# A larger first block, early multiplications and a split last tile in a gated mix of attention and a gMLP block

## The chip, the cores and the metric

The kernel runs on one core of a Trainium2 chip. The metric is device time in microseconds (us), the median of several executions of the same program. A profile is one further execution, with every instruction and every DMA packet recorded. The engines are named as in the profile: PE (TensorE, the matrix multiplications), PEld (its weight loads), DVE (VectorE), ACT (ScalarE), POOL (GpSimd) and SP (SyncE). In this kernel SP issues every transfer. The matrix engine writes only to PSUM, which is used as eight banks of 128 x 512 float32 numbers.

## What is computed

There are 2048 tokens (S) of width 1024 (D), in bfloat16. Two branches of the same input x are mixed by a gate of each token:

```python
x = A_x
g = _sigmoid((x * gate_w).sum(-1, keepdims=True))
a = _A_ref(x, A_wqkv, A_wo)      # dilated sliding-window attention, 32 heads of 32, 8 positions each
b = _B_ref(x, B_w_in, B_w_sp, B_b_sp, B_w_out)
return g * a + (1 - g) * b

# _B_ref
z = _gelu(jnp.einsum('bsd,df->bsf', x, w_in))        # w_in: 1024 x 3584, Fh = 1792
z1 = z[..., :Fh].copy()
z2 = _layernorm(z[..., Fh:], axis=-1)
g = jnp.einsum('ts,bsf->btf', w_sp, z2) + b_sp[None, :, None]
return jnp.einsum('bsf,fd->bsd', z1 * g, w_out)
```

## The kernel before, in words

Work is tiled by 128 tokens (row tiles i = 0 to 15) and by 128 of the 1024 input features (k tiles kt = 0 to 7). `xT` holds x transposed, features on the partitions. `w2` holds the second half of w_in in four column blocks c of 512, 512, 512 and 256 columns (`ZC`, `ZW`), and the gate's weights as one more column of the last block.

The order of PE's work is the order in which the program writes it:

1. Row tiles 0 and 1 are transposed on PE (`z2_pair`, L230), because x arrives in plain layout for these two; DVE and ACT copy the results into `xT` (L234, L236). Then these two row tiles are multiplied with column block 0 of `w2` (L215), interleaved by pairs of k tiles so that each of four transfers of `w2` (L389, two k tiles of 512 columns, 256 KB) feeds four multiplications.
2. Row tiles 2 to 15 are multiplied with column block 0 (`z2_tile`). Their `xT` comes from transposing DMAs (L394), which SP issues after the transfers above.
3. The q, k and v projections of eight groups of four heads (L421); ACT copies the results out, SP stores them to DRAM and loads them back in the attention's layout.
4. The remaining z2 tiles (`z2_tile(i, c)` for c = 1 to 3, L441), with the sum of squares of each row tile on ACT (L443).
5. z1 by gelu (L463), stored to DRAM.
6. The spatial product (`g_chunk`, L477), two chunks, then alternately with `final_chunk` (L498 attention output times wo, L502 gated product times w_out), which mixes the two (ACT L505, DVE L506) and stores one output tile of 128 x 1024 (L509).

The attention itself runs on DVE (L257 to L296), beside all this. Its steps are placed into the program by a planner, `Beat`. Each stage of PE work reports its columns with `beat.run(cols)`, at 2360 columns a us; steps with a due time are emitted once the planner's clock has reached it. The attention's due times hang on the clock at the start of stage 3: `attention_steps(beat.now + QKV_US + 10.0)` (L410). At its end it loads wo (L348) and the first transposed attention outputs `oT` (L351), which stage 6 needs. SP works through its instructions in order, so a transfer that waits holds back those behind it.

PSUM tiles are taken in turn from one pool of eight, whatever their use.

Of the kernel before, what the change touches and what calls it, by code (L numbers as in the profile page):

```python
# [10 lines left out]
F32 = mybir.dt.float32  # L11
BF = mybir.dt.bfloat16

P = 128
S = 2048
D = 1024
KT = D // P
# [8 lines left out]
FH = 1792  # L26
NF = FH // P
ZC = 512
ZW = (512, 512, 512, 256)
# [21 lines left out]
def kernel(  # L51
# [13 lines left out]
    nc = tc.nc  # L65
    x2 = A_x.rearrange("b s d -> (b s) d")
    out2 = out.rearrange("b s d -> (b s) d")

    apool = ctx.enter_context(tc.tile_pool(name="arena", bufs=1))
    sm = ctx.enter_context(tc.tile_pool(name="small", bufs=1))  # L70
    psum = ctx.enter_context(tc.tile_pool(name="psum", bufs=8, space=bass.MemoryType.PSUM))
# [4 lines left out]
    def reg(off, n):  # L76
        return arena[:, off:off + n]
# [3 lines left out]
    v_d = dpool.tile([NG, S + 16, C], BF, name="v_d")  # L81
    z1_d = dpool.tile([4, P, NF * 512], BF, name="z1_d")
    o_d = dpool.tile([S, D], BF, name="o_d")

    ident = sm.tile([P, P], BF, name="ident")
    make_identity(nc, ident[:])
# [3 lines left out]
    for jh in range(2):  # L90
        for w in range(W):
            n = min(8, max(0, 14 - 2 * w - 8 * jh))
# [4 lines left out]
    g_s = sm.tile([P, 16], F32, name="g_s")  # L97
    gl_s = sm.tile([P, 16], F32, name="gl_s")
    omg = sm.tile([P, 16], F32, name="omg")
# [17 lines left out]
    w_out_sb = reg(X_OFF, NF * D).rearrange("p (f n) -> p f n", f=NF)  # L117
# [5 lines left out]
    wo_sb = reg(A_OFF, KT * D).rearrange("p (k n) -> p k n", k=KT)  # L123
    oT_slots = [reg(A_OFF + 8192 + r * 1024, 1024).rearrange("p (k t) -> p k t", k=KT) for r in range(3)]
    ob_slots = [reg(A_OFF + 11264 + r * 1024, 1024) for r in range(3)]
    asb_slots = [reg(A_OFF + 14336 + r * 1024, 1024).bitcast(F32) for r in range(2)]
    w2 = reg(CD_OFF, KT * W2P).rearrange("p (k c) -> p k c", k=KT)
# [16 lines left out]
    win_v = B_w_in.rearrange("(k p) c -> p k c", p=P)  # L144
    wsp_v = B_w_sp.rearrange("(a t) s -> a t s", t=P)
    wo_v = A_wo.rearrange("(g h d) n -> g h d n", g=NG, h=HG, d=DH)
    sync = nc.sync
# [38 lines left out]
    beat = Beat()  # L186
# [19 lines left out]
    def z2_tile(i, c):  # L206
        N = ZW[c] + 1 if c == 3 else ZW[c]
        ps = psum.tile([P, 512], F32, name="ps", tag="ps")
        for kt in range(KT):
            z2_mm(ps, i, c, kt, N)  # L210
        z2_out(ps, i, c)
        beat.run(KT * N)

    def z2_mm(ps, i, c, kt, N):
        nc.tensor.matmul(ps[:, 0:N], xT[:, kt, i * P:(i + 1) * P], w2[:, kt, ZC * c:ZC * c + N],  # L215
                         start=(kt == 0), stop=(kt == KT - 1))

    def z2_out(ps, i, c):
        n = ZW[c]
        nc.scalar.activation(z2[:, i, ZC * c:ZC * c + n], ps[:, 0:n], ACT.Gelu_apprx_tanh,  # L220
                             accum_out=s1[:, 4 * i + c:4 * i + c + 1])
        if c == 3:
            nc.scalar.copy(gl_s[:, i:i + 1], ps[:, n:n + 1])

    def z2_pair():
        for i in range(2):
            for h in range(2):
                pt = psum.tile([P, 4, P], BF, name="pt", tag="ps")
                for k in range(4):
                    nc.tensor.transpose(pt[:, k, :], xn[:, i, (4 * h + k) * P:(4 * h + k + 1) * P], ident[:])  # L230
                for k in (0, 2):
                    dst = xT[:, 4 * h + k:4 * h + k + 2, i * P:(i + 1) * P]
                    if k == 0:
                        nc.vector.tensor_copy(dst, pt[:, k:k + 2, :])  # L234
                    else:
                        nc.scalar.copy(dst, pt[:, k:k + 2, :])  # L236
        pair = [psum.tile([P, 512], F32, name="ps", tag="ps") for _ in range(2)]
        for kk in range(0, KT, 2):
            for i in range(2):
                for kt in (kk, kk + 1):  # L240
                    z2_mm(pair[i], i, 0, kt, ZW[0])
        for i in range(2):
            z2_out(pair[i], i, 0)
        beat.run(2 * KT * ZW[0])

    L = att_L
    L4 = L[:].rearrange("p (a w n) -> p a w n", a=2, w=W, n=32)
# [102 lines left out]
    def load_oT(a):  # L350
        sync.dma_start_transpose(oT_slots[a % 3], o_d[a * P:(a + 1) * P, :])  # L351

    def stats(i):
        sl = slice(i - 3, i + 1)
        s1v = s1[:, 4 * (i - 3):4 * (i + 1)].rearrange("p (i c) -> p i c", c=4)
        nc.vector.tensor_reduce(mean[:, sl], s1v, AX.X, ALU.add)
        nc.vector.tensor_scalar(mean[:, sl], mean[:, sl], 1.0 / FH, None, ALU.mult)
        nc.vector.tensor_tensor(var[:, sl], mean[:, sl], mean[:, sl], ALU.mult)
        nc.vector.scalar_tensor_tensor(var[:, sl], s2[:, sl], 1.0 / FH, var[:, sl], ALU.mult, ALU.subtract)
        nc.vector.tensor_scalar(var[:, sl], var[:, sl], 0.0, EPS, ALU.max, ALU.add)  # L360
        nc.gpsimd.tensor_tensor(rstd[:, sl], var[:, sl], cm05[:, sl], ALU.pow)
        beat.on_vector(0.8)

    def norm(ii):
        nc.vector.tensor_scalar(z2[:, ii, :], z2[:, ii, :], mean[:, ii:ii + 1], rstd[:, ii:ii + 1],
                                ALU.subtract, ALU.mult)
        beat.on_vector(0.75)
# [17 lines left out]

    for i in range(2):
        sync.dma_start(xn[:, i, :], x_v[:, i, :])  # L387
    for kk in range(0, KT, 2):
        sync.dma_start(w2[:, kk:kk + 2, 0:ZC], win_v[:, kk:kk + 2, FH:FH + ZC])  # L389
    for i in range(2, 16):  # L390
        if i == 14:
            load_w(0, 3)
# [3 lines left out]
    load_wg(1)  # L396
    for t_d in (k_d, v_d):
        sync.dma_start(bass.AP(tensor=t_d.tensor, offset=t_d.offset, ap=[[16, P], [(S + 16) * C, NG], [1, 16]]), zeros[:])
    for c in range(1, 4):
        sync.dma_start(w2[:, :, ZC * c:ZC * c + ZW[c]], win_v[:, :, FH + ZC * c:FH + ZC * c + ZW[c]])  # L400
    sync.dma_start(w2[:, :, FH:FH + 1], gw_v)

    z2_pair()
    for i in range(2, 16):
        if i == 14:
            v_order(0)
# [6 lines left out]
    for g in range(NG):  # L413
# [3 lines left out]
        for j in range(NJ):  # L417
            ps = psum.tile([P, 512], F32, name="ps", tag="ps")
            for kt in range(KT):
                lhsT = _sub_ap(xT_flat, kt * S + j, [[NJ, P]])  # L420
                nc.tensor.matmul(ps[:, 0:3 * C].rearrange("p (t c) -> p t c", t=3), lhsT, wgt[:, 0:3, kt, :],  # L421
                                 start=(kt == 0), stop=(kt == KT - 1))
# [15 lines left out]
    load_w1(0)  # L438
    load_w1(1)
    for i in range(16):  # L440
        for c in range(1, 4):  # L441
            z2_tile(i, c)
        nc.scalar.activation(junk, z2[:, i, :], ACT.Square, accum_out=s2[:, i:i + 1])  # L443
        if i % 4 == 3:
            beat.at(beat.now + 6.0, lambda i=i: stats(i))
            for ii in range(i - 3, i + 1):
                beat.at(beat.now + 11.0, lambda ii=ii: norm(ii))
# [6 lines left out]
    for f in range(NF):  # L454
# [5 lines left out]
        for c in range(4):  # L460
            ps = psum.tile([P, 512], F32, name="ps", tag="ps")
            for kt in range(KT):
                nc.tensor.matmul(ps[:], w1[:, kt, (f % 4) * P:(f % 4 + 1) * P], xT[:, kt, 512 * c:512 * (c + 1)],  # L463
                                 start=(kt == 0), stop=(kt == KT - 1))
# [22 lines left out]
    def final_chunk(c):  # L487
        z1c = z1c_slots[c % 2]
        for aa in range(4):
            a = 4 * c + aa  # L490
            oT = oT_slots[a % 3]
            ob = ob_slots[a % 3]
            if a > 0 and a + 2 < 16:
                load_oT(a + 2)
            for n in range(2):
                psa = psum.tile([P, 512], F32, name="psa", tag="ps")
                for kt in range(KT):
                    nc.tensor.matmul(psa[:], oT[:, kt, :], wo_sb[:, kt, 512 * n:512 * (n + 1)],  # L498
                                     start=(kt == 0), stop=(kt == KT - 1))
                psb = psum.tile([P, 512], F32, name="psb", tag="ps")  # L500
                for f in range(NF):
                    nc.tensor.matmul(psb[:], z1c[:, f, aa * P:(aa + 1) * P], w_out_sb[:, f, 512 * n:512 * (n + 1)],  # L502
                                     start=(f == 0), stop=(f == NF - 1))
                asb = asb_slots[n]
                nc.scalar.activation(asb, psa[:], ACT.Copy, scale=g_s[:, a:a + 1])  # L505
                nc.vector.scalar_tensor_tensor(ob[:, 512 * n:512 * (n + 1)], psb[:], omg[:, a:a + 1], asb,  # L506
                                               ALU.mult, ALU.add)
                beat.run((KT + NF) * 512)
            sync.dma_start(out2[a * P:(a + 1) * P, :], ob)  # L509

    load_z1c(0)
    for aa in range(4):
# [7 lines left out]
    for aa in range(4):  # L520
        load_wsp(3, aa)
    beat.flush(1e9)
    final_chunk(0)
    load_z1c(2)
    g_chunk(2)
    final_chunk(1)
    load_z1c(3)
    g_chunk(3)
    final_chunk(2)
    final_chunk(3)  # L530

# [29 lines left out]
```

## Time and profile before

| what | value |
|---|---|
| median of 3 runs | 718.73 us (718.09 to 718.87) |
| profiled execution, its own time | 718.52 us |
| its span, first to last instruction | 716.7 us |
| PE busy | 709.1 us, 99% of the span |
| DVE, ACT busy | 414.2 us, 251.7 us |
| mean rate of the DMAs | 130 GB/s |
| PE idle before its first instruction | 3.6 us |
| last multiplication ends | 712.9 us from the span's start |

The span begins with the first instruction that the profile shows and ends with the last one; 1.8 us of the execution's own time lie around it. Where a group of multiplications gives a mean of 379 ns for 128 x 512, that is the time of one from issue to its modelled end; they overlap, and the distance from one start to the next is shorter. That distance, not the mean, is what a multiplication costs in a row of them.

### The profile page before, as it was taken

To read this page: it belongs to the slowest core of one execution; us is meant where nothing else is said; L and a number is where in the kernel's file an instruction comes from. 1 tells how busy PE (TensorE), PEld (TensorE's weight loads), DVE (VectorE), ACT (ScalarE), POOL (GpSimd) and SP (SyncE) were. 2 spreads that over 40 slices of the span, in tenths; PEclk is the share of its full clock that TensorE was granted. 3 is DMA by queue.
4 is the path that set the end of the run, shared out by engine and by line. 5 is a ranking of instruction groups with operands and counts; after the bars stand their busy time and mean duration, and the time that the engine had idled before them with its cause. 6 is when DMAs were issued, how large, how long until landed. Compare 5 with 4: busy or idle time off the path is not lost.

```text
span 716.7 us, 8882 instructions
## 1 busy us (share of the span) xinstructions
PE 709.1 (99%) x3600; PEld 400.2 (56%) x3600; DVE 414.2 (58%) x427; ACT 251.7 (35%) x482; POOL 11.5 (2%) x23
## 2 busy tenths in 40 slices
PE   7999999999999999999999999999999999999997
PEld 3488888888865554444444444444444444444443
DVE  0001979999999999999999996211222112221111
ACT  4444455444378894343522111111111111111111
POOL 1000000000000021000000000000000000000000
PEclk9999999999999999999999999999999999999999
DMA  9978687667681207953469764482400223002210
GB/s 212 178 205 232 144 205 180 162 152 176 176 247 55 85 6 206 265 189 119 142 211 278 267 118 138 84 146 59 133 1 0 54 55 113 1 1 59 59 45 29
DMA packets 177449, 92.93 MB, mean 130 GB/s; under 512 B 145024, under 2 KB 168576, under 8 KB 176896
## 3 DMA queue, kind: packets, MB, share of 16 engines
q1 hardware_dynamic: 177408, 92.36, 49.0%
q8 instruction: 28, 0.46, 0.3%
q14 instruction: 13, 0.11, 0.1%
HBM read 47.71 MB, written 28.38 MB: 106 GB/s over the span
## 4 chain that ended last, share of the span: by engine, by line
PE 99%; DMA 1%; SPq 0%; DVE 0%; issue 0%; DVEq 0%
PE ps L477 27%; PE ps L421 23%; PE ps L215 14%; PE psb L502 13%; PE ps L463 13%; PE psa L498 8%; DMA arena<-in_B_w_in_dram 1%; SPq L387 0%; DVE arena L506 0%; DVEq L506 0%
## 5 line engine op out<-in xcount | busy, mean ns | idle before, releaser
L477 PE MATMUL ps<-arena 128*128 128x512 bf16 x896 | 193.9, 379 | 0.0
L421 PE MATMUL ps<-arena 128*128 128x384 bf16 x1024 | 166.6, 326 | 0.0
L421 PEld LDWEIGHTS <-arena 128*128 128x128 bf16 x1024 | 147.6, 144 | 18.9
L477 PEld LDWEIGHTS <-arena 128*128 128x128 bf16 x896 | 87.7, 98 | 105.7
L502 PE MATMUL psb<-arena 128*128 128x512 bf16 x448 | 101.9, 379 | 0.0
L215 PE MATMUL ps<-arena 128*128 128x512 bf16 (+1 forms) x512 | 99.0, 356 | 0.2 <-DMA arena<-in_B_w_in_dram 0.2
L463 PE MATMUL ps<-arena 128*128 128x512 bf16 x448 | 96.9, 379 | 0.0
L506 DVE SCALAR_TENSOR_TENSOR arena<-psb,omg,arena 128x512 bf16<-128x512 f32 x32 | 24.0, 751 | 125.9 <-PE psb L502 125.9
L257 DVE TENSOR_TENSOR arena<-arena 128x8192 bf16<-128x8192 bf16 x16 | 70.8, 4423 | 43.8 <-DMA arena<-k_d 43.5
L424 ACT CAST arena<-ps 128x384 bf16<-128x384 f32 x128 | 60.4, 479 | 90.2 <-PE ps L421 86.8
L481 ACT CAST arena<-ps 128x512 bf16<-128x512 f32 x56 | 32.8, 585 | 164.4 <-PE ps L477 154.9
L260 DVE TENSOR_TENSOR arena<-arena 128x4096 bf16<-128x4096 bf16 (+1 forms) x64 | 77.6, 1213 | 2.0
L215 PEld LDWEIGHTS <-arena 128*128 128x128 bf16 x512 | 50.6, 99 | 48.3 <-issue 2.3
L502 PEld LDWEIGHTS <-arena 128*128 128x128 bf16 x448 | 43.9, 98 | 52.8
L463 PEld LDWEIGHTS <-arena 128*128 128x128 bf16 x448 | 43.8, 98 | 52.7
L482 DVE TENSOR_TENSOR arena<-arena 128x512 bf16<-128x512 bf16 x56 | 23.7, 422 | 83.7 <-ACT arena L481 83.7
L290 DVE TENSOR_TENSOR arena<-arena,att_A 128x8192 bf16<-128x8192 bf16 x16 | 70.7, 4421 | 0.2
L505 ACT ACTIVATE arena<-psa,g_s 128x512 f32<-128x512 f32 x32 | 22.0, 687 | 121.2 <-PE psa L498 121.2
L498 PE MATMUL psa<-arena 128*128 128x512 bf16 x256 | 60.5, 379 | 0.0
L465 ACT ACTIVATE arena<-ps 128x512 bf16<-128x512 f32 x56 | 33.2, 596 | 55.4 <-PE ps L463 55.3
L220 ACT ACTIVATE arena<-ps 128x512 bf16<-128x512 f32 (+1 forms) x64 | 34.3, 538 | 24.0 <-PE ps L215 23.8
L498 PEld LDWEIGHTS <-arena 128*128 128x128 bf16 x256 | 25.1, 98 | 30.2
(51 smaller groups left out, 252.5 us busy)
## 6 DMA issues: line engine op xcount, KB each, us to landing
arena<-k_d SPq DMA_DIRECT2D x8, 960.0 KB, 7.0
arena<-v_d SPq DMA_DIRECT2D x8, 960.0 KB, 4.7
z_d<-arena SPq DMA_DIRECT2D x14, 512.0 KB, 3.3
arena<-z_d SPq DMA_DIRECT2D x4, 1792.0 KB, 7.6
arena<-in_A_wqkv_dram SPq DMA_DIRECT2D x24, 256.0 KB, 4.5
arena<-in_B_w_in_dram SPq DMA_DIRECT2D x5, 1024.0 KB, 8.1
q_d<-arena SPq DMA_DIRECT2D x32, 128.0 KB, 2.1
k_d<-arena SPq DMA_DIRECT2D x32, 128.0 KB, 2.4
```

The costliest lines, as they stand in the source:

```text
L215: nc.tensor.matmul(ps[:, 0:N], xT[:, kt, i * P:(i + 1) * P], w2[:, kt, ZC * c:ZC * c + N], start=(kt == 0), stop=(kt == KT - 1))
L220: nc.scalar.activation(z2[:, i, ZC * c:ZC * c + n], ps[:, 0:n], ACT.Gelu_apprx_tanh, accum_out=s1[:, 4 * i + c:4 * i + c + 1])
L257: TT(prod.rearrange("p (w j c) -> p w j c", w=W, j=8, c=C), in0, in1, ALU.mult)
L260: return lambda: TT(pv[:, :, 0:half], pv[:, :, 0:half], pv[:, :, half:2 * half], ALU.add)
L290: TT(prod.rearrange("p (w j d h) -> p w j d h", w=W, j=8, d=DH, h=HG), in0, in1, ALU.mult)
L421: nc.tensor.matmul(ps[:, 0:3 * C].rearrange("p (t c) -> p t c", t=3), lhsT, wgt[:, 0:3, kt, :], start=(kt == 0), stop=(kt == KT - 1))
L424: nc.scalar.copy(st[:, j % 4, :], ps[:, 0:3 * C])
L463: nc.tensor.matmul(ps[:], w1[:, kt, (f % 4) * P:(f % 4 + 1) * P], xT[:, kt, 512 * c:512 * (c + 1)], start=(kt == 0), stop=(kt == KT - 1))
L465: nc.scalar.activation(z1s[:, c, :], ps[:], ACT.Gelu_apprx_tanh)
L477: nc.tensor.matmul(ps[:], z2[:, i, f * P:(f + 1) * P], wsp[:, i, :, :].rearrange("p a t -> p (a t)"), start=(i == 0), stop=(i == 15))
L498: nc.tensor.matmul(psa[:], oT[:, kt, :], wo_sb[:, kt, 512 * n:512 * (n + 1)], start=(kt == 0), stop=(kt == KT - 1))
L502: nc.tensor.matmul(psb[:], z1c[:, f, aa * P:(aa + 1) * P], w_out_sb[:, f, 512 * n:512 * (n + 1)], start=(f == 0), stop=(f == NF - 1))
```

## The change

It has three parts.

- **Early multiplications.** A tile of zeros (`warm`, 128 x 512) is written by DVE at the start; before anything else PE multiplies it six times into a PSUM tile that nobody reads.
- **The first block.** Row tiles 0 and 1 are multiplied with column blocks 0 and 1 together, in four PSUM banks (`z2_quad` in place of `z2_pair`), k tile by k tile. The weights come in eight transfers, one of 1024 columns for each k tile (256 KB each), in place of four; the later transfer of column block 1 is left out, and stage 4 leaves out c = 1 for row tiles 0 and 1. The planner is told of twice the columns.
- **The last output tile** (a = 15) is computed and stored in three pieces of 512, 256 and 256 columns, in place of two of 512 and one store.

```diff
+    warm = sm.tile([P, 512], BF, name="warm")
+    nc.vector.memset(warm[:], 0.0)
+
+    def warm_up(n):
+        pw = psum.tile([P, 512], F32, name="pw", tag="ps")
+        for _ in range(n):
+            nc.tensor.matmul(pw[:], warm[:, 0:P], warm[:], start=True, stop=True)
...
-    def z2_pair():
+    def z2_quad():
...
-        pair = [psum.tile([P, 512], F32, name="ps", tag="ps") for _ in range(2)]
-        for kk in range(0, KT, 2):
+        quad = [[psum.tile([P, 512], F32, name="ps", tag="ps") for c in range(2)] for i in range(2)]
+        for kt in range(KT):
             for i in range(2):
-                for kt in (kk, kk + 1):
-                    z2_mm(pair[i], i, 0, kt, ZW[0])
+                for c in range(2):
+                    z2_mm(quad[i][c], i, c, kt, ZW[c])
         for i in range(2):
-            z2_out(pair[i], i, 0)
-        beat.run(2 * KT * ZW[0])
+            for c in range(2):
+                z2_out(quad[i][c], i, c)
+        beat.run(2 * KT * (ZW[0] + ZW[1]))
...
-    for kk in range(0, KT, 2):
-        sync.dma_start(w2[:, kk:kk + 2, 0:ZC], win_v[:, kk:kk + 2, FH:FH + ZC])
+    for kt in range(KT):
+        sync.dma_start(w2[:, kt, 0:2 * ZC], win_v[:, kt, FH:FH + 2 * ZC])
...
-    for c in range(1, 4):
+    for c in range(2, 4):
         sync.dma_start(w2[:, :, ZC * c:ZC * c + ZW[c]], win_v[:, :, FH + ZC * c:FH + ZC * c + ZW[c]])
...
-    z2_pair()
+    warm_up(6)
+    z2_quad()
...
-        for c in range(1, 4):
+        for c in range(2 if i < 2 else 1, 4):
             z2_tile(i, c)
...
-            for n in range(2):
+            last = a == 15
+            for n0, nw in ((0, 512), (512, 256), (768, 256)) if last else ((0, 512), (512, 512)):
                 psa = psum.tile([P, 512], F32, name="psa", tag="ps")
                 for kt in range(KT):
-                    nc.tensor.matmul(psa[:], oT[:, kt, :], wo_sb[:, kt, 512 * n:512 * (n + 1)],
+                    nc.tensor.matmul(psa[:, 0:nw], oT[:, kt, :], wo_sb[:, kt, n0:n0 + nw],
                                      start=(kt == 0), stop=(kt == KT - 1))
...
-                asb = asb_slots[n]
-                nc.scalar.activation(asb, psa[:], ACT.Copy, scale=g_s[:, a:a + 1])
+                asb = asb_slots[n0 // nw % 2][:, 0:nw]
+                nc.scalar.activation(asb, psa[:, 0:nw], ACT.Copy, scale=g_s[:, a:a + 1])
...
-            sync.dma_start(out2[a * P:(a + 1) * P, :], ob)
+                if last:
+                    sync.dma_start(out2[a * P:(a + 1) * P, n0:n0 + nw], ob[:, n0:n0 + nw])
+            if not last:
+                sync.dma_start(out2[a * P:(a + 1) * P, :], ob)
```

More of the change, by code (lines that the diff above doesn't have):

```diff
@@ L501, in final_chunk @@
                 for f in range(NF):
-                    nc.tensor.matmul(psb[:], z1c[:, f, aa * P:(aa + 1) * P], w_out_sb[:, f, 512 * n:512 * (n + 1)],
+                    nc.tensor.matmul(psb[:, 0:nw], z1c[:, f, aa * P:(aa + 1) * P], w_out_sb[:, f, n0:n0 + nw],
                                      start=(f == 0), stop=(f == NF - 1))
-                asb = asb_slots[n]
-                nc.scalar.activation(asb, psa[:], ACT.Copy, scale=g_s[:, a:a + 1])
-                nc.vector.scalar_tensor_tensor(ob[:, 512 * n:512 * (n + 1)], psb[:], omg[:, a:a + 1], asb,
+                asb = asb_slots[n0 // nw % 2][:, 0:nw]
+                nc.scalar.activation(asb, psa[:, 0:nw], ACT.Copy, scale=g_s[:, a:a + 1])
+                nc.vector.scalar_tensor_tensor(ob[:, n0:n0 + nw], psb[:, 0:nw], omg[:, a:a + 1], asb,
                                                ALU.mult, ALU.add)
-                beat.run((KT + NF) * 512)
-            sync.dma_start(out2[a * P:(a + 1) * P, :], ob)
+                beat.run((KT + NF) * nw)
+                if last:
+                    sync.dma_start(out2[a * P:(a + 1) * P, n0:n0 + nw], ob[:, n0:n0 + nw])
+            if not last:
+                sync.dma_start(out2[a * P:(a + 1) * P, :], ob)
     load_z1c(0)
```

## The prediction

> **What bounds the kernel now.** I read the busy times first, then what PE waited for, then the chain of waits.
>
> ```profile
> PE 709.1 (99%) x3600; PEld 400.2 (56%) x3600; DVE 414.2 (58%) x427; ACT 251.7 (35%) x482; POOL 11.5 (2%) x23
> ```
>
> ```profile
> PE pt L230 <- DMA arena<-in_A_x_dram: 3.6, 1, 3.6
> PE ps L215 <- DMA arena<-in_B_w_in_dram: 0.2, 1, 0.2
> ```
>
> ```profile
> 1.64 3.96 DMA arena<-in_B_w_in_dram
> 5.65 29.48 PE ps L215 x128
> 35.13 166.40 PE ps L421 x1024
> 201.53 69.33 PE ps L215 x384
> 270.86 96.69 PE ps L463 x448
> 367.56 96.69 PE ps L477 x448
> ```
>
> PE waits twice in the whole span, 3.6 and 0.2 us, both at the start. From 5.65 us on, the chain is PE work without a hole, up to the last multiplication at 712.9. So the time is what PE has to do, plus the first 5.65 us, plus the 3.8 us behind it. The sums of work don't change (16 multiplications of 512 columns move from stage 4 into the first block); only the two ends can.
>
> A multiplication of 512 columns costs 96.69 / 448 = 0.2158 us (the L477 row). The 128 of the row at 5.65 should then take 27.6 us, not 29.48: 1.9 us are lost. Two stretches of PE's timeline, and the same two as a table of windows, show where:
>
> ```profile
> 3.59 1.89 PE L230 MATMUL pt<-ident,arena 128*128 128x128 bf16 x16 [3.59 <-DMA arena<-in_A_x_dram]
> 5.65 4.01 PE L215 MATMUL ps<-arena 128*128 128x512 bf16 x10 [0.17 <-DMA arena<-in_B_w_in_dram]
> ```
>
> ```profile
> 5.65:9.02 3.37, 3.37 (x9) 1.13 (x9) 1.00 1.20 296
> 9.50:12.95 3.45, 3.45 (x17) 1.57 (x16) 1.00 0.92 187
> ```
>
> The first window holds eight starts and the first instant of a ninth: 0.427 us from start to start. The second holds sixteen and a touch: 0.216. The granted clock reads 1.00 in both, so that column doesn't show it, but the first eight run at half speed, and each loses 0.211 us, 1.69 in all. The weight loads of the slow eight wait for "issue", not for a transfer.
>
> **Part 1, the early multiplications.** Removed: nothing. Added: one DVE write of 128 x 512, six multiplications. No such DVE write is in the trace; POOL's MEMSET of 128 x 512 took 0.53 us and of 128 x 128 0.19; I take 0.53 (the same shape), with 0.2 and 0.7 as ends. The other engines start at 0.73, so PE starts at about 0.73 + 0.53 + 0.2 = 1.5 and its six cost 6 x 0.427 = 2.56 us: to 4.0. Queued behind them on PE are the 16 transposes, released at 3.59 now; they slip by 0.4 and still run 16 x 0.107 = 1.7 us, to 5.7. The first weights land at 1.64 + 4.0 = 5.6, so the first useful multiplication slips by 0.1 (ends: 0 and 0.4). DVE's and ACT's copies of the transposes slip alike; nothing else is queued on either.
>
> What does it buy? PE turned fast at 9.0, 5.4 us after its first transpose and 3.4 after its first multiplication. After the end it turned slow again: the clock reads 1.00 up to 715.6 and 0.50 from 715.7. From 9.1 to 715.7 are 706.6 us. By itself the trace can't say whether the transposes count as work. The three runs speak for it: suppose that the turn needs a full stretch of the 3.4 us just read, and that such stretches follow one another on a grid that ignores the program. If only multiplications counted, it would fall between 9.06 and 12.5, and the time between about 718.5 and 720.2 (0.5 us for each us of delay). The runs are at 718.09, 718.73 and 718.87, and the profile at 718.52. If transposes count, the turn falls between 7.0 and 10.4, and the time between 717.5 and 719.2, which holds all four. I take that. With work on PE from 1.5 on, the turn then falls between 4.9 and 8.3. If the grid lies as in the profile it comes at 5.7, and all 1.69 are saved. Over all positions: loss before (8.7 - 5.65) / 2 = 1.5, loss after 0.5 (half of the mean delay behind 5.65: 0.78 of the positions lie behind it, by 1.3 on average), so 1.0 saved. I take 1.4, between the two, with 0 and 1.7 as ends.
>
> [...]
>
> **Part 2, the first block.** PE does 32 multiplications where it did 16: the same 0.2158 each, taken from stage 4. Each 256 KB still feeds four. At full speed four take 0.86 us. The four transfers now land 4.0, 4.2, 4.4 and 4.7 us behind their issues 0.5 apart, that is at 5.6, 6.3, 7.0 and 7.8: one each 0.72. So PE isn't starved: 0. The upper end is the rate of 241 GB/s that the window 7 to 8 us shows: 1.09 us each, the last at 13.2 and the block's end 1.4 late.
>
> SP: eight issues of 0.47 in place of four, so the 14 transposing DMAs are issued some 2 us later, and those behind them on SP too (wqkv, the zeros). The first lands at 3.65 + 5.1 = 8.8 now, 1.0 after the last weights. With the last weights at 5.6 + 7 x 0.72 = 10.6 it lands at 11.6. Needed: after 32 fast multiplications, 5.75 + 6.9 = 12.65. The later ones are issued one per 1.35 us and used one per 1.73. Cost 0, with a cover of about 1 us.
>
> The planner's clock is 8192 columns further at stage 3, so the attention stands 3.45 us later against stages 5 and 6. Its last loads now land at 445.0 + 8.4 = 453.4 (first `oT`), needed at 464.25: a cover of 10.9, of which 7 stay; one more gated tile on DVE (0.85) leaves 6. In stage 4, ACT has about 3.4 us of work for row tiles 0 and 1 against 2.6 us of PE: 0.8 late twice, which free PSUM banks cover. The dropped transfer of column block 1 frees 1 MB of DMA at 33 us that nobody waits for.
>
> **Part 3, the last tile.** PE: 22 multiplications of 512 become 44 of 256. Those of 257 columns cost (69.33 - 256 x 0.2158) / 128 = 0.110, so 22 x (2 x 0.110 - 0.2158) = +0.1. Behind the last multiplication lie DVE and a store:
>
> ```profile
> 713.00 0.75 DVE L506 SCALAR_TENSOR_TENSOR arena<-psb,omg,arena 128x512 bf16<-128x512 f32 x1 [4.01 <-PE psb L502]
> ```
>
> ```profile
> L509 SPq DMA_DIRECT2D out_dram<-arena x1: 332/332/332, 713.8 to 713.8; - x1
> DMA to landing us min/median/max: 2.0/2.0/2.0
> ```
>
> With 256 columns DVE takes between 0.38 (half) and 0.75; ACT's gelu of 512 and 256 columns took 0.59 and 0.38, that ratio gives 0.48: -0.27. The store of 64 KB in place of 256 lands after 2.0 at most and, at the 400 GB/s of the x load, 0.5 sooner at best: I take -0.3. The second piece reuses the first's buffer of ACT's result; DVE is done with it 0.8 us after PE, ACT comes to it 0.9 after: no wait. SP's three stores lie 2.4 us apart and find it idle. Together -0.5 (+0.1 to -0.8).
>
> **Sum.** -1.4 + 0.1 - 0.5 = -1.8 us. Against the profiled execution (718.52; 0.2 below the median) with the grid as there it is -2.1, 716.4; against the median 716.9.
>
> **Rivals.**
> - *The clock comes no sooner.* Transposes don't count, or the early work is broken off. Against it speaks the spread of the runs, which is thin. Only the tail is left: 718.73 + 0.1 - 0.5 = 718.3.
> - *The transfers end the first block.* The second transposing DMA held SP for 2.5 us, where others take 1.3, so the queue pushes back while weights are on their way. If the first transposing DMA gets in only once the weights are through (10.6) and needs its 5.1, row tile 2 lands at 15.7 and PE waits 3.05. Above 11.6 + 1.05 each us costs one; above 14.5 the change loses. Worst: 718.73 - 1.8 + 3.05 = 720.0. Against it: the first issue now goes in behind four weights unhindered (1.36).
> - *The attention arrives late.* If DVE loses over 6 us more to waits on z1 loads or SP's order, stage 6 starts late and pays all above it; at 10 lost, 718.73 - 1.8 + 4 = 720.9. Against: DVE's own waits for z1 are 9.0 us today, two times, and no PE wait shows.
>
> **Numbers.** 0.2% is 1.44 us, about what a measurement of this kernel can tell from none. Likeliest case 0.68 (715.9 to 717.9: three quarters of it beyond 717.29), first rival 0.19, second 0.08, third 0.05. Faster: 0.51 + 0.04 from lucky positions in the first rival; slower: half of the last two with their worst ends, 0.08; the rest same. The range from 715.9 to 718.7 leaves out the last two and some of the edges.
>
> **What will show it.** Right: fast starts (0.216) from about 6 on; PE without a wait between 5.8 and the end; a tail of 3.2 us in place of 3.8. Wrong: 0.427 up to 9 or later; a PE wait for x at row tile 2, or for `oT` at about 463.

## The result: 0.28% faster, and where the profile after shows it

The changed kernel takes 716.5 us (median of 8 runs, 715.74 to 717.06) against 718.8 (8 runs, 717.74 to 719.73). The ratio of the runs is 0.9972, 95% interval 0.9963 to 0.9982, that is 1.3 to 2.7 us less; the two medians lie 2.3 us apart. The forecast was 716.9 (715.9 to 718.7). Two single slow executions of the experiments below (1076.69 us at a granted clock of 0.66, and 2268.41 us at a granted clock of 1.00, whose cause is not known) are left out of medians and spreads, and the turn of the clock is not read from the profile of the first (three early multiplications).

The profiled execution took 716.54 us, its span 714.7 in place of 716.7. The page's busy times and PE's waits of the kernel after:

```profile
PE 706.6 (99%) x3577; PEld 402.0 (56%) x3628; DVE 414.0 (58%) x429; ACT 251.3 (35%) x483; POOL 11.0 (2%) x23
```

```profile
PE ps L223 <- DMA arena<-in_B_w_in_dram: 1.2, 1, 1.2
PE pw L91 <- DVE warm L86: 1.2, 1, 1.2
```

PE still waits only at the start: for the tile of zeros, and for the first weights. (3577 multiplications are shown, 3628 weight loads: some records of multiplications are missing.) There is no wait at row tile 2 and none at `oT`. PE's timeline of the kernel after (start, length, count), and one of its windows (PE busy and count, granted clock, DMA share, GB/s):

```profile
1.19 2.74 PE L91 MATMUL pw<-warm 128*128 128x512 bf16 x6 [1.19 <-DVE warm L86]
3.72 1.12 PE L238 MATMUL pt<-ident,arena 128*128 128x128 bf16 x16
6.05 5.99 PE L223 MATMUL ps<-arena 128*128 128x512 bf16 x27 [1.20 <-DMA arena<-in_B_w_in_dram]
```

```profile
6.05:9.02 2.97, 2.97 (x14) 1.00 1.05 392
```

Two readings. The 16 transposes take 1.12 us, not 1.89: the clock turned while they ran. The trace's clock record (it lists from when to when which share of the clock was granted; where it holds nothing, the column of the windows prints 1.00) begins at 3.85 us, against 9.11 before, and from there the distance between transposes falls from 0.107 to 0.056 us. And 2.97 us hold almost 14 useful multiplications (0.216 from start to start), where a like window held 8.

The tail of the kernel after, in its timeline, and its last store:

```profile
711.76 0.48 DVE L517 SCALAR_TENSOR_TENSOR arena<-psb,omg,arena 128x256 bf16<-128x256 f32 x1 [1.92 <-PE psb L513]
712.27 0.33 SPq L521 DMA_DIRECT2D out_dram<-arena  x1
```

```profile
L521 SPq DMA_DIRECT2D out_dram<-arena x1: 333/333/333, 712.3 to 712.3; - x1
...
DMA to landing us min/median/max: 1.6/1.6/1.6
```

The two profiled spans differ by 1.98 us, and the pieces add up: the first useful multiplication starts 0.40 later (6.05 for 5.65); from there to DVE's last instruction it is 705.71 for 707.35, that is -1.64 (-1.69 for the eight slow multiplications, +0.06 for the 44 narrow ones); DVE -0.27; the store -0.44; the rest -0.03.

### The profile page after: what moved, and what is told of

It is laid out like the page before. It is cut to its first block, busy times and chain, and to the rows that moved or that the text cites. A ratio compares the mean times of both kernels' runs of the same rounds, so it can differ in the third digit from the quotient of the medians.

```text
span 714.7 us, 8897 instructions
## 1 busy us (share of the span) xinstructions
PE 706.6 (99%) x3577; PEld 402.0 (56%) x3628; DVE 414.0 (58%) x429; ACT 251.3 (35%) x483; POOL 11.0 (2%) x23
## 4 chain that ended last, share of the span: by engine, by line
PE 98%; DMA 1%; issue 0%; SPq 0%; DVE 0%; DVEq 0%
PE ps L487 27%; PE ps L431 23%; PE ps L223 14%; PE ps L473 13%; PE psb L513 13%; PE psa L509 8%; DMA arena<-in_B_w_in_dram 1%; SPq L396 0%; DVE arena L517 0%; DVEq L517 0%
## 5 line engine op out<-in xcount | busy, mean ns | idle before, releaser
L513 PE MATMUL psb<-arena 128*128 128x512 bf16 (+1 forms) x455 | 101.3, 372 | 0.3
L223 PE MATMUL ps<-arena 128*128 128x512 bf16 (+1 forms) x501 | 96.7, 352 | 1.8 <-DMA arena<-in_B_w_in_dram 1.2
L517 DVE SCALAR_TENSOR_TENSOR arena<-psb,omg,arena 128x512 bf16<-128x512 f32 (+1 forms) x33 | 24.3, 735 | 125.4 <-PE psb L513 113.4
L516 ACT ACTIVATE arena<-psa,g_s 128x512 f32<-128x512 f32 (+1 forms) x33 | 22.2, 674 | 122.3 <-PE psa L509 118.2
L509 PE MATMUL psa<-arena 128*128 128x512 bf16 (+1 forms) x259 | 60.2, 372 | 0.4
```

The costliest lines, as they stand in the source:

```text
L509: nc.tensor.matmul(psa[:, 0:nw], oT[:, kt, :], wo_sb[:, kt, n0:n0 + nw], start=(kt == 0), stop=(kt == KT - 1))
L513: nc.tensor.matmul(psb[:, 0:nw], z1c[:, f, aa * P:(aa + 1) * P], w_out_sb[:, f, n0:n0 + nw], start=(f == 0), stop=(f == NF - 1))
```

## Experiments

The theory: the early work turns PE's clock up sooner, the tail gives the rest, the block gives nothing. Times beside each run are against the kernel before on the same chip.

### Early multiplications alone

```diff
 # the kernel before
+    warm, warm_up() as in the change
+    warm_up(6)
     z2_pair()
```

> The kernel before, with the tile of zeros and its six early multiplications and nothing else of the change. Theory (the clock is what the change bought): fast starts (0.216 us) before the first useful multiplication or soon behind it, 1.2 to 1.7 us less than before, about 717.3. Rival (the larger first block or its transfers bought it): no more than 0.4 us less than before, 718.4 or above. The trace shows besides when the first weights land with the old transfers of two k tiles by 512 columns: at 5.6 as before if the 0.4 us that they came later after the change lie in the new shape, at 6.0 if they don't.

717.1 us (11 runs, 716.79 to 717.55) against 718.63; ratio 0.9982, 0.9973 to 0.9990. By the ratio that is 1.3 us less, with bounds of 0.7 and 1.9; by the medians it is 1.5. PE's timeline of this run:

```profile
1.19 2.74 PE L91 MATMUL pw<-warm 128*128 128x512 bf16 x6 [1.19 <-DVE warm L86]
3.72 1.85 PE L238 MATMUL pt<-ident,arena 128*128 128x128 bf16 x16
5.71 1.76 PE L223 MATMUL ps<-arena 128*128 128x512 bf16 x7
```

Here the clock record begins at 5.38, at the end of the transposes (still 1.85 us), and all useful multiplications are fast. The first weights land at 5.67, in the old shape of transfer.

The runs show a second thing. The kernel before spread over 3.2 us on this chip (29 runs, 716.95 to 720.12), this one over 0.76 (11 runs). The two kernels that follow have 11 runs each on the same chip and no early work, and spread over 1.81 and 1.57. So most of the variation from run to run seems to go with the moment of the turn; that is inferred from these spreads, since only a profile shows its turn.

### The larger block alone

```diff
 # the changed kernel
-    warm_up(6)
     z2_quad()
...   # and the last tile as before
```

> The kernel before, with the block of two row tiles by two column blocks and its eight transfers, without early multiplications and with the old last tile. Theory: the block by itself brings nothing; PE does the same multiplications at the same pace and starts when the first weights land: 0 to 0.4 us more than before, 718.8 to 719.2, with 8 slow starts at 0.427 us or more of them. Rival (the block is what bought it): 1 us or more less than before, 717.8 or below.

718.25 us (11 runs) against 718.63; ratio 0.9996, 0.9987 to 1.0005: no difference, though the median lies below the 718.8 to 719.2 that were expected. Its waits on PE and a window:

```profile
PE pt L230 <- DMA arena<-in_A_x_dram: 3.4, 1, 3.4
PE ps L215 <- DMA arena<-in_B_w_in_dram: 0.6, 1, 0.6
```

```profile
5.91:8.43 2.52, 2.52 (x7) 1.00 0.98 351
```

Six starts in 2.52 us, nearly all 0.427 apart: the slow stretch is there as before, until 8.75, where the clock record begins. The block only moves work.

### The split tail alone

```diff
 # the kernel before
+            for n0, nw in ((0, 512), (512, 256), (768, 256)) if last else ((0, 512), (512, 512)):
...   # final_chunk as in the change
```

> The kernel before with the last output tile in three pieces, nothing else. From the trace after: DVE's last instruction 0.75 to 0.48, the last store 2.00 to 1.56 us, 44 multiplications of 256 columns for 22 of 512 at +0.07: 0.64 us less than before, 718.1. Rival (the tail is hidden or the short store is no faster here): within 0.2 us of before. The time between the last multiplication's start and the span's end tells them apart more sharply than the medians.

717.65 us (11 runs) against 718.63; ratio 0.9988, 0.9979 to 0.9997. The interval holds the expected 0.64 us and twice that; the trace is sharper. DVE's last instruction in it:

```profile
712.17 0.48 DVE L507 SCALAR_TENSOR_TENSOR arena<-psb,omg,arena 128x256 bf16<-128x256 f32 x1 [1.92 <-PE psb L503]
```

From its start to the end of the span (715.31) it is 3.14 us, where the kernel before took 3.72 (713.00 to 716.72): 0.58 less. The 44 narrow multiplications take back 0.06, so the tail gives 0.5 us here. In the profile after the same sum gives 0.7 (2.97 in place of 3.72, and 0.06 back).

This profile also held a case by chance. Its turn came at 7.01 (the start of the clock record), though PE had begun at 3.56 and on useful multiplications only at 5.96:

```profile
3.56 1.89 PE L230 MATMUL pt<-ident,arena 128*128 128x128 bf16 x16 [3.56 <-DMA arena<-in_A_x_dram]
5.96 1.52 PE L215 MATMUL ps<-arena 128*128 128x512 bf16 x4 [0.51 <-DMA arena<-in_B_w_in_dram]
```

One us of multiplications was enough, if the transposes ahead of them counted.

### Do transposes count as work?

```diff
 # the changed kernel
-            nc.tensor.matmul(pw[:], warm[:, 0:P], warm[:], start=True, stop=True)
+            for k in range(4):
+                nc.tensor.transpose(pw[:, k, :], warm[:, k * P:(k + 1) * P], ident[:])
...
-    warm_up(6)
+    warm_up(5)
```

> The changed kernel, with 20 transposes of the zeros in place of the six multiplications: PE is as busy from about 1.9 us on, but with transposes alone up to the first weights at about 6.0. If transposes count as work for the clock: fast starts from the first or second useful multiplication on, time within 0.4 us of the changed kernel, 716.3 to 716.9. If only multiplications count: the first eight or more useful multiplications at 0.427 us, 1.3 to 2 us above the changed kernel, 717.8 or above.

716.19 us (7 runs, 716.07 to 716.74) against 718.63; ratio 0.9970, 0.9959 to 0.9981: a little below the 716.3 to 716.9 expected if transposes count. PE's timeline and a window of this run:

```profile
1.79 2.29 PE L92 MATMUL pw<-ident,warm 128*128 128x128 bf16 x20 [1.79 <-POOL ident masks.py:199]
3.87 1.76 PE L239 MATMUL pt<-ident,arena 128*128 128x128 bf16 x16
5.53 3.74 PE L224 MATMUL ps<-arena 128*128 128x512 bf16 x15
```

```profile
5.53:8.24 2.71, 2.71 (x14) 1.00 0.98 323
```

Nothing but transposes ran on PE up to 5.53, and the clock record begins at 5.34; the last two transposes start 0.056 us apart, those before 0.107. So transposes count, as this kernel issues them (the trace shows them as multiplications with `ident`); no other form of transpose on PE was run here.

### Half of the early work

```diff
 # the changed kernel
-    warm_up(6)
+    warm_up(3)
```

> The changed kernel with three early multiplications in place of six: 1.28 us of early work, then a hole of about 0.8 us until x lands at 3.3, transposes to about 5.0, a hole to about 5.6 to 6.0. Theory (the clock goes by the share of a stretch of 3.4 us in which PE works, transposes included; 78% was enough in the profile after, 55% was not in that before): the turn comes between about 4.6 and 8, so part of the gain goes, 0.2 to 0.8 us above the changed kernel, 716.7 to 717.3. Rival (any early work wakes the clock): same time as the changed kernel within 0.2 us, turn before 5.

717.65 us (median of 10 runs, 716.23 to 718.58) against 718.63; by medians 1.2 us above the changed kernel on the same chip (below), more than expected. The spread says how: some runs are as fast as the changed kernel, others are slow almost like the kernel before. With three there is a hole of 0.8 us on PE until x lands; that the turn comes before the weights in some runs and behind them in others fits the spread, but no profile with three at full clock shows it. That any early work wakes the clock in every run is out.

### Weights sooner: two ways that failed

Before the first weights PE idles for 1.2 us in the profile after. Could they land sooner?

```diff
 # a: the changed kernel, first two k tiles issued by ACT
     for kt in range(KT):
-        sync.dma_start(w2[:, kt, 0:2 * ZC], ...)
+        q = nc.scalar if kt < 2 else sync
+        q.dma_start(w2[:, kt, 0:2 * ZC], ...)
 # b: the changed kernel, k tile 0 ahead of x
     for kt in range(KT):
         sync.dma_start(w2[:, kt, 0:2 * ZC], ...)
+        if kt == 0:
+            ...   # x's two tiles
```

> The changed kernel, with the weights of the first two k tiles issued by ACT at the start and the other six by SP as now, so that they don't queue behind x. PE's hole ahead of the first useful multiplication (1.2 us in the profile after, none to 0.6 in the others) should go. Theory (the first weights are late because they are issued third and touched late, not because the transfers lack rate): first weights land at 4.5 to 5.2, x up to 0.5 us later than now, the first useful multiplication starts at 4.9 to 5.3, 0.4 to 1.0 us below the changed kernel, 715.5 to 716.1. Rival (the rate is the limit, 512 KB more ahead of x's second tile): x lands later by as much as the weights land earlier, time within 0.2 us of the changed kernel.

> The changed kernel, with the weights of the first k tile issued by SP ahead of x, nothing else. Theory as for the two queues: the wait of some 2 us between the last x packet's time and the first weights' landing is a cost of the first touch of that tensor, and now lies beside the wait for x: weights at 3.5 to 4.5, x 0.5 to 0.7 us later (3.9 and 4.6), first useful multiplication at about 5.2 to 5.5, 0.2 to 0.8 us below the changed kernel. Rival (the transfers behind x, second and third k tile, now come late and PE waits for those instead): the first useful multiplication starts earlier, but PE waits at the second or third k tile, time within 0.2 us.

Both expectations were missed. With two queues: 718.44 us (11 runs) against 718.63, ratio 0.9996 (0.9987 to 1.0005), so nearly all the gain is gone, the tail's share too. With the weights first: 716.86 (11 runs, 716.12 to 719.05); ratio 0.9982, 0.9972 to 0.9993. PE's timelines, first with two queues, then with the weights first:

```profile
1.19 2.74 PE L91 MATMUL pw<-warm 128*128 128x512 bf16 x6 [1.19 <-DVE warm L86]
4.70 2.20 PE L238 MATMUL pt<-ident,arena 128*128 128x128 bf16 x16 [0.77 <-DMA arena<-in_A_x_dram]
6.70 1.06 PE L223 MATMUL ps<-arena 128*128 128x512 bf16 x2
```

```profile
4.23 0.75 PE L238 MATMUL pt<-ident,arena 128*128 128x128 bf16 x8 [0.31 <-DMA arena<-in_A_x_dram]
5.63 0.62 PE L238 MATMUL pt<-ident,arena 128*128 128x128 bf16 x8 [0.64 <-DMA arena<-in_A_x_dram]
6.09 1.24 PE L223 MATMUL ps<-arena 128*128 128x512 bf16 x5
```

With two queues x lands at 4.7 and 5.8, not at 3.3 and 3.9; the useful work starts 0.65 later than in the profile after, and its first four multiplications are slow, the fifth in part. This profile has no clock record, but the starts show the turn: they are 0.427 apart up to 8.40 and 0.216 from 8.75 on, which puts it at about 8.7. The clock records of the other profiles have two lengths, 3.41 us apart (last section). Counted back from 8.7 in steps of 3.41, which assumes that such steps run on ahead of the turn, a stretch that ended without a turn lies from 1.84 to 5.25, and the window of it reads:

```profile
1.84:5.25 3.41, 2.64 (x11) 1.00 0.94 319
```

PE was busy for 2.64 us of it, and the clock did not turn. The late start (0.65) and the slow multiplications (about 1.0) together are the 1.6 us by which this profiled execution (718.17) is slower than that of the change (716.54). Ten of the eleven runs lie at 718.1 or above, so most of them seem to miss the early turn, though only this one profile shows it. With the weights first, the runs fall into two groups, six of 716.1 to 716.9 and four of 718.5 to 719.1 with one between; the profile is one of the first group.

The reason that I had given, a cost of the first touch of the weights, falls as well. With the weights first they land at 3.56 and x's first tile at 4.19, and now x's second tile is the late one, at 5.58. It is again the third transfer, and it comes 1.4 us behind the second.

### Count, or bytes?

```diff
 # a: the changed kernel, x's two tiles in one transfer
-    for i in range(2):
-        sync.dma_start(xn[:, i, :], x_v[:, i, :])
+    sync.dma_start(xn, x_v[:, 0:2, :])
 # b: in four
     for i in range(2):
-        sync.dma_start(xn[:, i, :], x_v[:, i, :])
+        for h in range(2):
+            sync.dma_start(xn[:, i, 512 * h:512 * (h + 1)], x_v[:, i, 512 * h:512 * (h + 1)])
```

> The changed kernel with x's first two tiles in one transfer of 512 KB in place of two of 256. It asks what makes the third transfer late by about 1.4 us, whether it is the weights (as in the kernel before and after) or x (with the weights first). If it is the count of transfers: the first weights, now second, land at 4.6 to 4.9, the second k tile's 2 us behind them; PE starts on useful work at 5.6 to 5.8 and may wait at the second k tile; time 0 to 0.4 us below the changed kernel. If it is the bytes moved (512 KB) or the moment (3.5 to 5 us): first weights at 5.5 to 6.3 as now, x complete at about 3.9, the transposes end at about 5.7: time 0 to 0.3 us above the changed kernel.

> The changed kernel with x's first two tiles in four transfers of 128 KB. If the count of transfers makes the third late: the third quarter of x lands about 1.4 us behind the second, at about 4.5 to 5, PE has a hole within the transposes, weights at about 6; time 0 to 1 us above the changed kernel. If it is the bytes or the moment: four landings from about 2.9 to 4.1 at even distance, the stall with the first weights as now; time within 0.3 us of the changed kernel.

In one: 716.29 us (6 runs) against 718.44, ratio 0.9965 (0.9953 to 0.9977). In four: 717.05 (12 runs, 716.50 to 718.88), ratio 0.9983 (0.9974 to 0.9992). The changed kernel did not run on this chip, so the two can't be set against it closely; its median on another chip is 716.46 (below). With one transfer x lands at 4.18 and the weights, now second, at 5.03 and 5.98: the first k tile comes sooner than with x in two or four transfers, and the next is 0.95 behind it. With four, x lands at 2.83, 3.50, 3.83 and 5.02 and the first weights at 6.11; the third quarter, expected late, is not. So the late transfer is not simply the third, nor simply the one behind 512 KB. Transfers of 256 KB that follow undisturbed land 0.6 to 0.8 us apart; one between 3.5 and 6.3 us lands 0.95 to 2.3 behind the one before it, in a place that moves. What causes it stays open.

### The changed kernel again, and one attempt to better it

> The changed kernel itself, beside the three above on the same chip: 716.2 to 716.8, 1.7 to 2.4 us below the kernel before. What it adds is a second profile: the turn of the clock between about 3.8 and 7.2, the first weights between 5.4 and 6.1.

716.46 us (6 runs, 716.34 to 716.90), ratio 0.9969 (0.9957 to 0.9980). In this second profile the turn came at 6.06 and the first weights landed at 6.32, later than expected:

```profile
1.19 2.74 PE L91 MATMUL pw<-warm 128*128 128x512 bf16 x6 [1.19 <-DVE warm L86]
3.72 1.91 PE L238 MATMUL pt<-ident,arena 128*128 128x128 bf16 x16
6.36 1.02 PE L223 MATMUL ps<-arena 128*128 128x512 bf16 x4 [0.73 <-DMA arena<-in_B_w_in_dram]
```

The turn is 2.2 us later than in the first profile, and the profiled time only 0.27 longer (716.81), which is about what the later weights cost (useful work from 6.36 in place of 6.05): the clock was up before the weights were there.

```diff
 # the changed kernel, x's two tiles in one transfer
-    warm_up(6)
+    warm_up(7)
```

> x's first two tiles in one transfer, and seven early multiplications in place of six, so that they end at about 4.15, when x lands (4.18 in the run before this one). Theory: no hole on PE from 1.2 to the first useful multiplication at about 5.4 to 5.9; the clock turns before it or within 0.5 us of it in every run; 716.0 to 716.4, 0 to 0.5 us below the changed kernel beside it, and a spread of the runs under 1.3 us. Rival: the hole of 0.3 us mattered to nothing; the same as with six, 716.3.

> The changed kernel beside the one above, on the same chip, to compare the two: 716.2 to 716.8 us, with a spread of its runs of 0.5 to 1.3 us.

716.61 us (6 runs, 716.06 to 717.53; ratio 0.9967) and 716.24 for the changed kernel (5 runs, 716.13 to 716.79; ratio 0.9964), both against 718.90. With seven no hole was left on PE, as planned (transposes from 4.15 to 5.86), and nothing was won, in the median or in the spread: the transposes ended after the first weights (4.79), and the turn came at 6.26. No version tried here is clearly below the changed kernel.

The third profile of the changed kernel, from this last run, shows something that the first two do not. Its turn came at 4.21, its first weights at 5.72, and then the third k tile landed only at 7.80, 1.42 us behind the second:

```profile
5.76 1.89 PE L223 MATMUL ps<-arena 128*128 128x512 bf16 x8 [0.75 <-DMA arena<-in_B_w_in_dram]
7.84 6.42 PE L223 MATMUL ps<-arena 128*128 128x512 bf16 x28 [0.19 <-DMA arena<-in_B_w_in_dram]
```

The eighth useful multiplication starts at 7.27 and the ninth at 7.84, 0.57 later where 0.216 is usual: the block's transfers cost this execution 0.35 us.

## Why the prediction was right, step by step

- **What bounds the kernel.** Right: the two ends alone moved. In the profile after no PE wait appeared in between. The first `oT` landed at 458.1 (issued at 451.17, 7.0 us to landing) and was needed at 462.8: of the cover of 10.9 us 4.7 are left, where 6 had been worked out.
- **The clock, -1.4 (0 to -1.7).** Right: 1.3 by the ratio and 1.5 by the medians (early multiplications alone), 1.69 between the two profiles. That transposes count had been taken from the spread of three runs, thin evidence; the run with transposes alone shows it.
- **When it turns.** Wrong in the step "the turn needs a full stretch of the 3.4 us". That, and the grid, were the author's supposition. The turn came at 3.85, outside of the 4.9 to 8.3 given. Counted back from each turn in steps of 3.41 us (an estimate: the records show such a step from turn to turn, not ahead of the turn), the stretch that ended in it (0.44 to 3.85) held 2.66 us of work, 78%. In the kernel before, a stretch with 1.94 us of work (2.29 to 5.70), 57%, did not turn it, and neither did the one with 2.64 us, 77%, in the run with two queues. So a full stretch was not needed here, but whether PE's busy time is the measure stays open: it would need a threshold between 77 and 78%, and the profile's ends of multiplications are modelled, so that these shares are not exact to a per cent. The wrong step cost nothing, and that was luck: in the profile after the weights were not there before 6.01, and any turn up to then saves the same.
- **The early work's own cost, +0.1.** DVE's write took 0.27 us, not 0.53, PE started at 1.19, not 1.5, and the transposes slipped by 0.13, not 0.4. The first useful multiplication came 0.40 later all the same, because the weights did: 6.01 for 5.61. The two shapes of transfer don't explain it: in the old one the first weights landed at 5.61, 5.67 and 5.92, in the new one at 6.01, 5.87, 5.49, 6.32 and 5.72, so the ranges overlap, and a cost of the new shape is not shown. The prediction had no term for this variation, which is 0.8 us wide.
- **The block, 0.** Right in the profile after and by the medians of the block alone; the transposed x for row tile 2 landed at 11.7 (11.6 worked out), needed at 12.95. In the third profile of the changed kernel the block lost 0.35 us to a late k tile. "One each 0.72" had been read from four transfers that followed evenly; here one came 1.42 behind the one before it.
- **The tail, -0.5.** DVE -0.27 as worked out, the store -0.44 (taken: 0.3, end 0.5), the narrow multiplications +0.06 (taken: 0.1): -0.65, and with what is left behind the store -0.7; in the run with the tail alone -0.5. From the modelled end of the last multiplication the tail is 3.1 us in place of 3.8, where 3.2 had been forecast.
- **Sum.** -2.1 had been worked out for the profiled execution with the grid as before, and -1.8 on the median. Measured: -1.98 and -2.3 (-2.0 by the ratio). On the profiled execution two misses cancel in part: the useful work began 0.40 later, not 0.1, and the tail gave more than 0.5.

The rivals fell: the clock did come sooner, PE did not wait for row tile 2, the attention did not arrive late.

## What to carry to other kernels

Where a kernel's PE is busy from end to end, look at the distance between its first multiplications: if it is twice that of the later ones (here 0.427 us for 0.216), work that needs no input, placed where PE would wait for its first load, can take the slow stretch away, as it did in the profile after (0.216 from the first useful multiplication on). Half as much was too little here: it gave up 1.2 of the 2.2 us, most of what the early work had brought, as 0.5 to 0.7 of the 2.2 are the tail's. What delays the first loads can undo it: with two queues x landed 1.4 and 1.9 us later, a hole of 0.77 opened on PE, and nearly all of the gain was gone. A hole once the clock was up did no harm here: in the profile after PE idled for 1.2 us right before the useful work and went on at 0.216 from start to start. A spread of run times can itself be a reading: on one chip it was 0.76 us over 11 runs with the early work, 1.6 to 1.8 over 11 without.

## What the runs showed of the hardware that was not expected

- Transposes on PE, as this kernel issues them, turn the clock up as multiplications do: in the run with early transposes, with nothing else on PE until 5.53 us, it was up at 5.34.
- From turn to turn the clock kept to a grid in these runs. Its record at full speed runs from 3.85 to 713.82 in the profile after, 709.972 us, and from 9.11 to 715.67 before, 706.559. The profiles of the other runs at full clock, where they hold the record, show one of these two lengths and no third; they differ by 3.413 us and are 208.0 and 207.0 times that. Whether the grid runs on ahead of the first turn is not shown. The program alone does not set the moment: in three profiles of the changed kernel, with PE's first multiplication at 1.19 each time, it came at 3.85, 6.06 and 4.21.
- Shortly after the start one transfer comes late: it lands 0.95 to 2.3 us behind the one before it, where others follow 0.6 to 0.8 apart, whichever tensor it carries. In some profiles a second gap follows, such as that from 6.38 to 7.80 above. Between 3.5 and 6 us single packets take up to 1022 ns in the profile before and up to 907 in that after, where the median of their size is 46 (1 KB) and 84 (2 KB). The cause was not found.
